# Sparse attention and two gated layers on one core: the planned order of the layers planned anew

## The chip, the cores and the metric

The kernel runs on one core of a Trainium2 chip. The metric is the device time of one execution in microseconds (us); of several executions the median is given. The profile comes from one further execution, and its times are that execution's own.

## The reference

Attention keeps, in each row, the scores within `tau` of the row's maximum, and its output goes through two gated layers, all in float32:

```python
scores = scale * np.matmul(q, k.transpose(0, 1, 3, 2))       # 4 x 8 heads, 576 x 576, head size 64
thresh = np.max(scores, axis=-1, keepdims=True) - tau
scores = np.where(scores >= thresh, scores, -1000000000.0)
...
x = np.ascontiguousarray(attn_out.transpose(0, 2, 1, 3)).reshape(B * S, H * D)    # 2304 x 512
h = x @ w_in                                                 # 512 x 2048
g = h * np.tanh(log1p(exp(h)))
x = g @ w_out
g = x @ w_gate                                               # 512 x 1536
x = (g * sigmoid(g) * (x @ w_val)) @ w_out2
```

## The kernel before

**Two parts.** `attention` works on 16 pairs of heads, about 16.4 us each. `moes` then computes the two feed-forward layers in 30 blocks: layer 1 has 4 groups of hidden columns, layer 2 has 6, and each group meets three row chunks r = 0, 1, 2 of 768 tokens. So blocks 0 to 11 are layer 1 and blocks 12 to 29 layer 2, and a new group of weights is needed at blocks 0, 3, 6, ... 27. All matmuls are in a float32 that is split into a high and a low part (L515 and L519 for weights, L609 and L610 for inputs, L815 and L818 for hidden values g), three products for one.

**The first product of a block** (L783, into PSUM `ha` and `hb`) is done with seven products in place of eight, by sums of quarters of the weights and of the input. The inputs' seven pieces are `B11`, `T1` and so on. They are made once for each layer and chunk (a subtraction at L604, the split at L609 and L610, in tile `xp`), stored to DRAM (L613) and, for later groups, fetched again (L748). ACT copies results out of PSUM (L794: `s` and `u`), DVE adds them (L804 and others: `c`), ACT applies the nonlinearity (L827), and the split gives `g`. **The second product** (L907 in layer 1, L909 in layer 2, into PSUM `y`) is added into `acc` in SBUF, by ACT as a copy in a layer's first group (L923) and by DVE after that (L925).

**A weight's way** (`Weights.convert`). Weights lie in DRAM as 64-bit words of float64 bits. A block of 128 x 512 is loaded into `raw` (two slots, DMA on SP's queue, L480). ACT reads each word's two halves (`cu` L484, `cl` L488), DVE takes the sign (L492) and puts sign and body together (L495, `cn`), and GpSimd adds the rest (L498). Two such blocks, a pair, are then combined on DVE (L546, `sb`) into the sums that the seven products need and split into `wa`, `wb` and `wc` (three slots each); a block of the second product's weights becomes `wo` (six slots). The weights of the first two pairs are made during attention.

**What sets the order.** No engine's order is written by hand. `Plan` gets every operation with an engine, a cost, what it comes after, which slots it takes and frees, and a rank. `Plan.order` runs a list scheduler: at each step the engine that can start earliest takes, among the operations ready within `wait` (`MWAIT` in `moes`) of that time, the one of lowest rank. Operations are then issued in order of planned start. Engines and SP's DMA queue execute in that order, so an operation whose input comes later than planned holds up all behind it. In attention the ranks are numbers in `RANK` and the order is strict (an engine takes them by rank alone). In `moes` a matmul of block b has as its rank its place in time `R` (blocks laid end to end by the matmuls' lengths); evacuations have `R - 40`, piece preparations `R - LEAD`, fetches `R - FETCH` (60). Conversions are ranked by `prepare(bn)`, spread from the start of block bn - 3 to that of block bn:

```python
def rank(s, at=at):
    return T0 + PREP[0] + (T1 - T0 + PREP[1]) * at / n + PRANK.get(s, 0)
```

Here `at` counts the blocks of weights of the group, 0 to n - 1, and `s` is the step (`l` load, `h` high part, `o` low part, `s` sums). In the plan a load costs 1.6 us and its data is there 1.9 us after that; a conversion's add on GpSimd costs 1.1 us.

**The last v.** In attention each pair's v is loaded (L79) into the tile `vn`, of which there is one: the load waits until the product with the pair before's v (`av`, L177) is done.

Of the kernel before, what the change touches and what calls it, by code (L numbers as in the profile page):

```python
# [8 lines left out]
F32 = mybir.dt.float32  # L9
# [7 lines left out]
P = 128  # L17
# [26 lines left out]
def attention(tc, cst, q, k, v, x, beside, S=576):  # L44
# [9 lines left out]
    NP = q.shape[0]  # L54
# [8 lines left out]
    pw = ctx.enter_context(tc.tile_pool(name="a_w", bufs=2, reuse_waits="tile"))  # L63
# [6 lines left out]
    def mine(nm, h):  # L70
        return slice(64, 640) if nm == "k" and h == 0 else slice(0, 576)

    def load(p, nm):
        src = dict(q=q, k=k, v=v)[nm][p]
        if nm == "v":
            t = pw.tile([P, 10, 64], F32, tag="vn", name=f"vn{p}", bufs=SLOTS["vn"])
        else:
            t = pn.tile([P, KW], F32, tag="n", name=f"{nm}n{p}", bufs=SLOTS["n"])[:, 0:src.shape[1]]
        nc.sync.dma_start(out=t, in_=src)  # L79
        st[p][nm + "n"] = t  # L80
# [185 lines left out]
    turns = []  # L266
# [5 lines left out]
    plan = Plan(SLOTS, WAIT)  # L272
    for p in range(NP):
# [17 lines left out]
            op("ACT", .573 + .053 * (nm == "k"), inputs, nm, "hi", key=(nm, "hi"), after=[("q", "scale") if nm == "q" else ("k", "load")], take=[nm])  # L291
            op(*(("Pool", 1.4 + .15 * (nm == "k"), inputs, nm, "lo", nc.gpsimd) if p else ("DVE", .75, inputs, nm, "lo", nc.vector)), key=(nm, "lo"), after=[(nm, "hi")], free=["n"])
        op("Pool", .8, tails, key=("t",), after=[("q", "stack", 1) if p else ("q", "lo", 1)], take=["qt"], free=["q"] * (p > 0))
        op("DMA", 1.3, load, "v", key=("v", "load"), take=["vn"])
        for nm, cost in (("q", 1.3), ("k", 2.6)) * (p > 0):
            for h in range(2):
                op("DMA", cost, stack, nm, h, key=(nm, "stack", h), after=[(nm, "lo"), ("q", "stack", 0)][:2 if (nm, h) != ("q", 0) else 1], take=["stk"] * ((nm, h) == ("q", 0)))
        for i in range(9):
            c, h = divmod(i, 2)
            made = [(y, "stack", z) for y in "qk" for z in ([h] if i < 8 else [0, 1])] if p else [("q", "lo", h if i < 8 else 1), ("k", "lo")]  # L300
            op("PE", .53 if p and i < 8 else .81, scores, i, key=("S", i), after=made + [("t",)] * (i == 8), take=["s"], free=["k", "qt", "stk"] if i == 8 else [])
            op("DVE", .68, rowmax, i, key=("R", i), after=[("S", i)] + [("R", 0)] * (i > 0), take=["sm"] * (i == 0))
            op("Pool", .26, thresh, i, key=("H", i), after=[("R", i)])
            op("ACT", .7, expo, i, key=("E", i), after=[("R", i)], take=["e"])
            op("DVE", .8, mask, i, key=("M", i), after=[("E", i), ("H", i)] + [("M", i - 1)] * h, take=["pp"] if h == 0 else [], free=["s", "e"])
            for m0, n in (((0, 3),), ((3, 3), (6, 3)))[h] if i < 8 else ((0, 4), (4, 2)):
                g = turns[p, "T", next(small)]
                op("PE", .11 * n, trans, c, m0, n, key=("T", c, m0), after=[("M", i)], take=[g] + ["pt"] * (m0 == 0 and c in (0, 2)), free=["pp"] * (m0 == (6 if c < 4 else 4)))
                op("ACT", .365 if c < 4 else .54 if m0 == 0 else .21, evac, c, m0, n, key=("V", c, m0), after=[("T", c, m0)], free=[g])
            if i in (3, 8):  # L310
                u = int(i == 8)
                op("Pool", .26, added, u, key=("P", u), after=[("M", 3)] if u == 0 else [("M", 7), ("M", 8)])
                op("DVE", .2, recip, u, key=("Q", u), after=[("P", u)])
                op("Pool", .38 + .2 * u, rwide, u, key=("rw", u), after=[("Q", u)], take=["rw"], free=["sm"] * u)
                g = turns[p, "T", next(small)]
                op("PE", .22 + .22 * u, rbc, u, key=("B", u), after=[("rw", u)], take=[g], free=["rw"])
                op("ACT", .31, rcopy, u, key=("C", u), after=[("B", u)], take=["rs"], free=[g])
                ready = [("V", y, z) for y in ((0, 1), (2, 3))[u] for z in (0, 3, 6)] + [("V", 4, 0), ("V", 4, 4)] * u + [("v", "load")]
                for n, (j0, j1) in enumerate(PARTS):
                    end = j1 == 5  # L320
                    op("PE", (.432, .538)[u] * (j1 - j0), av, u, j0, j1, key=("A", u, n), after=ready, take=[] if n else [turns[p, "A", u]], free=(["pt"] + ["vn"] * u) * end)
                    ready = [("A", u, n)]
                op("DVE", .335 + .067 * u, xout, u, key=("x", u), after=[("C", u)] + ready, free=[turns[p, "A", u], "rs"])

# [7 lines left out]
class Plan:  # L332
# [37 lines left out]
    def order(self, ops, strict):  # L370
        made = {o["key"]: o for o in ops}
        took = {x: o for o in ops for x in o["take"]}
        gave = {x: o for o in ops for x in o["free"]}
        for o in ops:
            o["t"], o["then"] = 0.0 if strict or o["eng"] != "DMA" else AHEAD, []
        for o in ops:
            before = [(made[x], True) for x in o["after"] if x not in self.given]
            for x, k in o["take"]:
                if (x, k - 1) in took:
                    before.append((took[x, k - 1], False))  # L380
                if k >= self.slots[x]:
                    before.append((gave[x, k - self.slots[x]], True))
            o["left"] = len(before)
            for y, late in before:
                y["then"].append((o, late))
# [7 lines left out]
        while True:  # L393
# [20 lines left out]
                ready[e].remove(o)  # L414
            n += 1
            o["t"], o["at"] = t, n
            clock[e] = t + o["cost"]
            if e == "PE":
                clock[e] += TURN * (turn != (o["key"][1] == "A"))
                turn = o["key"][1] == "A"  # L420
            for y, whole in o["then"]:
                if whole:
                    y["t"] = max(y["t"], clock[e] + self.LAT[e][y["eng"]])
                else:
                    y["t"] = max(y["t"], t)
                y["left"] -= 1
                if not y["left"] and not tight(y):
                    ready[y["eng"]].append(y)
# [16 lines left out]
AHEAD = -20.0  # L445
# [3 lines left out]
AFTER = 10, 20  # L449
TURN = 0.16  # L450
KW = 640
SLOTS = dict(raw=2, wcu=1, wcl=2, wcn=3, sb=1, wa=2, wb=2, wc=2, xo=1, sm=4, s=3, g=2, e=4, pp=3, pt=2, rw=4, rs=3, q=2, k=2, qt=2, vn=1, stk=2, n=2)

PERIOD = 16.3760

# [4 lines left out]
class Weights:  # L460
# [9 lines left out]
            had = self.fixed.setdefault(nm, [])  # L470
            had.append(pool.tile([P, *shape], F32R, name=f"{nm}{len(had)}"))

    def convert(self, plan, pool, src, key, rank, cost=1.0, wait=(), into=None):
        nc, V = self.nc, self.nc.vector
        m, j, rows = src
        raw, up, low, n = plan.new("raw"), plan.new("wcu"), plan.new("wcl"), plan.new("wcn")
# [24 lines left out]
        for s, (eng, t, fn, deps, take, free) in dict(  # L501
            l=("DMA", 1.6 * cost, load, "", [raw], []),
            a=("ACT", .52 * cost, rebias, "l", [up], []),
            b=("ACT", .52 * cost, rest, "l", [low], []),
            c=("DVE", .335 * cost, sign, "l", [n], []),
            d=("DVE", .602 * cost, body, "abc", [], [raw, up]),
            x=("Pool", 1.1 * cost, whole, "bd", [], [low]),
        ).items():
            plan.op(eng, t, fn, K(s), [K(y) for y in deps] + list(wait) * (s == "l"), take, free, rank(s))
        return n  # L510

    def split(self, plan, key, tile, src, dst, n, low, rank, after, take=(), free=()):
# [107 lines left out]
def moes(tc, cp, acc, W, early, where, w_in, w_out, w_gate, w_val, w_out2, out):  # L620
# [36 lines left out]
    def prepare(bn):  # L657
# [15 lines left out]
        n = sum(2 if x[0] == "pair" else 1 for x in order)  # L673
        at = 0
        for what, q, x in order:
            def rank(s, at=at):
                return T0 + PREP[0] + (T1 - T0 + PREP[1]) * at / n + PRANK.get(s, 0)
            if what == "pair":
                ns = [W.convert(plan, pm, src, key, rank, into=pr) for src, key in x]
                weights["u", L, q] = W.combine(plan, pm, ("u", L, q), [key for _, key in x], ns, SENG, WLOW, rank)  # L680
                at += 2
            else:
                src, key = x
                nn = W.convert(plan, pm, src, key, rank if bn or at > 1 else lambda s: FIRST if s == "l" else rank(s), into=pr)
                weights[key] = W.out(plan, pm, key, nn, WLOW, rank)
                at += 1

    n1 = [("E", 1, 3, 2, q, i) for q in layers[1][-1] for i in range(4)]
    for bn, b in enumerate(blocks):
# [38 lines left out]
        for i, (k, q) in enumerate(seq):  # L728
# [3 lines left out]
            if q == g[0]:  # L732
# [8 lines left out]
                if new:  # L741
                    new.turn(plan, piece, PENG, ready, R - LEAD)
                    new.split(plan, piece, room, PLOW, ready, R - LEAD, 1, [xp])
                    new.store(plan, piece, room, R)
                    got = ("x", L, r, piece, "")
                else:
                    def fetch(room=room, piece=piece, L=L, r=r):
# [51 lines left out]
            def summed(nm, src, held, key, deps, free, q=q, tiles=tiles):  # L799
# [5 lines left out]

                S[nm, q] = t
                plan.op("DVE", dS(C), go, key, deps, [t], [S[held, q], *free], R)

            def split(nm, j, s, after, q=q, tiles=tiles):
                g_ = plan.new("g")  # L810
# [44 lines left out]
            elif k == 4:  # L855
# [4 lines left out]
                else:  # L860
                    def times(q=q, tiles=tiles):
                        V.tensor_tensor(out=tiles["c11", q], in0=tiles["A", q], in1=tiles["c11", q], op=ALU.mult)

                    plan.op("DVE", dS(C), times, ("V", *B, q, 0), [(*e, 3), K(4, q)], [], [ha[q]], R)
                    split("c11", q, 0, [("V", *B, q, 0)])
            elif k == 2:
                summed("c11", "B", "s1", ("c11", *B, q), [K(2, q), ("s1", *B, q)], [hb[q]])
# [10 lines left out]
        for s in (1, 0):  # L878
            ys = {}
            for jj, d, c0, c1 in [(jj, d, c0, c1) for jj, d in loop for c0, c1 in (((0, 256), (256, 512)) if ending and s == 0 and d == 2 else ((0, 512),))]:  # L880
# [51 lines left out]
                else:  # L932
                    after.append(("S", L, gi - 1, r, s, d))
                plan.op("ACT" if b["first"] else "DVE", aS(n_) if b["first"] else dS(n_), total_, key, after, [], [ys[d]] * (c1 == 512), R - 40)
                if b["last"] and L == 2:
                    def store(d=d, s=s, r=r, c0=c0, c1=c1):
                        t0 = 2 * C * r + C * s + P * d
# [8 lines left out]
FETCH = 60  # L946
FIRST = -1000
STAGED = (2, 0),
SLATE = 0
LEAD = 15  # L950
MWAIT = 0.06
MSLOTS = dict(ha=2, hb=2, y=4, xp=6, wa=3, wb=3, wc=3, wo=6, raw=2, wcu=2, wcl=2, wcn=3, sb=1, s1=2, u2=2, s5=2, c=4, g=9)
LAG = {1: .85, 2: .9}
PREP = (-5.0, -10.0)
PRANK = dict(l=-6, h=0, o=0)
PIECE = dict()
GLOW = {1: "DVE", 2: "DVE"}
SENG, WLOW, PENG, PLOW = "DVE", "DVE", "DVE", "DVE"
# [118 lines left out]
```

## Time and profile before

| | us |
|---|---|
| median of 3 runs | 1090.65 |
| lowest and highest | 1089.6, 1091.18 |
| the profiled execution's own time | 1085.61 |
| its span, first to last instruction | 1083.7 |
| busy: TensorE, DVE, ACT, GpSimd | 1059.2, 765.5, 651.2, 278.4 |
| granted TensorE clock | 1.000 of 2.4 GHz throughout |

PE is TensorE (PEld its weight loads), POOL is GpSimd, SP the queue that issues the DMAs. The first 281 us of the span are attention, the rest `moes`. Times within the trace count from the span's start. L12 is line 12 of the kernel before; tile names stand as out<-in.

### The profile page before, as it was taken

The page shows a single profiled execution, that of the slowest core. Times are in us where ns is not written, and L with a number is a line of the kernel's source. Part 1 is how long each engine was busy: PE and PEld are TensorE (multiplying, and loading weights), DVE is VectorE, ACT ScalarE, POOL GpSimd, SP SyncE. Part 2 cuts the span into 40 slices and gives each one's busy share as a digit, 9 for nine tenths or more (in the row PEclk, how much of TensorE's full clock was granted, in tenths as well). Part 3 has the DMA queues.
Part 4 walks back from the last instruction along what each step waited for, and adds up shares of the span by engine and source line. Part 5 has one row for each costly group of instructions (what it writes and reads, how often), then busy time and mean ns, then how long its engine had stood idle before and what let it go on. Part 6 is the DMA issues. An engine that isn't in the chain of part 4 may idle for free.

```text
span 1083.7 us, 17927 instructions
## 1 busy us (share of the span) xinstructions
PE 1059.2 (98%) x6358; PEld 970.0 (90%) x6358; DVE 765.5 (71%) x1445; ACT 651.2 (60%) x1313; POOL 278.4 (26%) x467
## 2 busy tenths in 40 slices
PE   6999999999999999999999999999999999999998
PEld 5777777777789999999999999898999999999997
DVE  7888988888686574466377677867487585775645
ACT  6899888887686764355356456656255354453331
POOL 5576877763240110031022002112011020110000
PEclk9999999999999999999999999999999999999999
DMA  5777767763966766576577497789788788887793
GB/s 151 193 189 216 189 166 220 205 200 102 363 242 259 250 239 204 182 273 239 175 246 255 161 337 272 278 291 323 242 292 309 241 316 281 277 293 239 235 304 128
DMA packets 66330, 259.47 MB, mean 239 GB/s; under 512 B 8768, under 2 KB 9024, under 8 KB 66240
## 3 DMA queue, kind: packets, MB, share of 16 engines
q1 hardware_dynamic: 66240, 258.31, 71.9%
q8 instruction: 51, 0.84, 0.3%
q14 instruction: 39, 0.32, 0.1%
HBM read 193.99 MB, written 37.75 MB: 214 GB/s over the span
## 4 chain that ended last, share of the span: by engine, by line
PE 84%; DVE 5%; DMA 3%; ACT 3%; POOL 2%; issue 1%; DVEq 0%; SPq 0%; POOLq 0%; ACTq 0%
PE ha L783 20%; PE y L907 16%; PE hb L783 15%; PE y L909 13%; PE av L177 7%; PE tg L154 6%; PE s L92 5%; DMA raw<-in_dram 2%; PE s L101 2%; DVE sm L109 1%; DVE g L818 1%; PE rg L202 1%; POOL cn L498 1%; DVE c L804 1%; POOL xo L610 1%
## 5 line engine op out<-in xcount | busy, mean ns | idle before, releaser
L498 POOL TENSOR_TENSOR cn<-cn,cl 128x512 int32<-128x512 int32 x68 | 102.5, 1509 | 633.4 <-DVE cn L495 520.6
L907 PE MATMUL y<-g,wo 128*128 128x384 f32 x1152 | 228.5, 334 | 4.1 <-ACT acc L923 3.6
L907 PEld LDWEIGHTS y<-g,wo 128*128 128x128 f32 x1152 | 202.1, 188 | 5.4 <-ACT acc L923 4.6
L909 PE MATMUL y<-wo,g 128*128 128x512 f32 (+1 forms) x654 | 167.4, 392 | 1.5 <-DVE acc L925 0.8
L925 DVE TENSOR_TENSOR acc<-y,acc 128x512 f32<-128x512 f32 (+2 forms) x163 | 100.0, 624 | 92.6 <-PE y L909 59.8
L783 PE MATMUL ha<-xp,wb 128*128 128x384 f32 x720 | 138.9, 335 | 1.1 <-ACT u L794 1.1
L909 PEld LDWEIGHTS y<-wo,g 128*128 128x128 f32 x654 | 120.3, 188 | 21.4 <-ACT xp L609 1.1
L783 PE MATMUL hb<-xp,wb 128*128 128x384 f32 x720 | 138.9, 335 | 0.5 <-ACT s L794 0.5
L783 PEld LDWEIGHTS ha<-xp,wb 128*128 128x128 f32 x720 | 126.5, 188 | 4.9 <-ACT u L794 1.9
L783 PEld LDWEIGHTS hb<-xp,wb 128*128 128x128 f32 x720 | 126.1, 188 | 2.9 <-ACT s L794 1.4
L818 DVE TENSOR_TENSOR g<-c,g 128x384 fp32r<-128x384 f32 x168 | 102.0, 610 | 30.5 <-ACT g L815 30.5
L127 DVE SCALAR_TENSOR_TENSOR pp<-s,sm,e 128x576 f32<-128x576 f32 x144 | 115.1, 813 | 10.9 <-ACT e L119 6.1
L815 ACT CAST g<-c 128x384 fp32r<-128x384 f32 x168 | 85.9, 512 | 53.2 <-DVE c L851 28.3
L109 DVE TENSOR_REDUCE sm<-s 128x1 f32<-128x576 f32 x144 | 106.6, 751 | 15.0 <-PE s L92 12.0
L827 ACT ACTIVATE c<-c 128x384 f32<-128x384 f32 x144 | 75.6, 525 | 60.9 <-DVE c L804 60.5
L119 ACT ACTIVATE e<-s,sm 128x576 f32<-128x576 f32 x144 | 105.7, 754 | 5.3 <-DVE sm L109 4.4
L154 PE MATMUL tg<-idf,pp 128*128 128x128 f32 x656 | 102.3, 280 | 2.8 <-DVE pp L127 1.7
L160 ACT COPY pt<-tg 128x384 f32<-128x384 f32 x192 | 87.3, 489 | 27.7 <-PE tg L154 26.6
L92 PE MATMUL s<-stk 128*128 128x320 f32 x480 | 93.0, 316 | 0.7 <-issue 0.5
L794 ACT COPY u<-ha 128x384 f32<-128x384 f32 x60 | 28.8, 480 | 103.2 <-PE ha L783 103.2
L154 PEld LDWEIGHTS tg<-idf,pp 128*128 128x128 f32 x656 | 73.1, 141 | 18.6 <-ACT e L119 5.8
L177 PE MATMUL av<-pt,vn 128*64 128x256 f32 (+1 forms) x640 | 84.7, 411 | 0.0
(95 smaller groups left out, 1555.0 us busy)
## 6 DMA issues: line engine op xcount, KB each, us to landing
raw<-in_dram SPq DMA_DIRECT2D x68, 512.0 KB, 5.5
xp<-x20T SPq DMA_DIRECT2D x24, 768.0 KB, 5.7
xp<-x21T SPq DMA_DIRECT2D x20, 768.0 KB, 5.5
xp<-x22T SPq DMA_DIRECT2D x20, 768.0 KB, 5.9
xp<-x20B SPq DMA_DIRECT2D x18, 768.0 KB, 5.8
xp<-x10T SPq DMA_DIRECT2D x16, 768.0 KB, 5.2
xp<-x21B SPq DMA_DIRECT2D x15, 768.0 KB, 5.8
xp<-x22B SPq DMA_DIRECT2D x15, 768.0 KB, 5.9
```

Source lines behind the costliest of these rows:

```text
L92: nc.tensor.matmul(out=s[:, c0:c0 + n], lhsT=d["stk"][:, 0, q0:q0 + P], rhs=d["stk"][:, w, k0:k0 + n], start=w == 1, stop=w == 2)
L109: nc.vector.tensor_reduce(out=d["nm"][:, i:i + 1], in_=d["s", i], op=ALU.max, axis=AX.X, negate=True)
L119: nc.scalar.activation(out=e, in_=d["s", i], func=AF.Exp, bias=d["nm"][:, i:i + 1])
L127: nc.vector.scalar_tensor_tensor(out=d["pp", c][:, 576 * h:576 * h + 576], in0=d["s", i], scalar=d["th"][:, i:i + 1], in1=d["e", i], op0=A ...
L154: nc.tensor.transpose(g[:, 128 * m:128 * m + 128], d["pp", c][:, o:o + 128], idf)
L177: nc.tensor.matmul(out=d["av", u][64 * h:64 * h + 64, 0:n], lhsT=d["vn"][:, 5 * h + j], rhs=d["pt", u][:, 5 * h + j if j < 4 else 4, 0:n], ...
L498: nc.gpsimd.tensor_tensor(out=self.n[key], in0=self.n[key], in1=self.l[key], op=ALU.add)
L783: nc.tensor.matmul(out=tiles[bank, q], lhsT=w[:, a, w0 + P * d:w0 + P * d + P], rhs=x[:, z, d], start=k in (1, 5, 2) and d == 0 and y == 0 ...
L818: (V if GLOW[L] == "DVE" else nc.gpsimd).tensor_tensor(out=tiles["g", j, s][:, 1], in0=tiles[nm, q], in1=f(tiles["g", j, s][:, 0]), op=ALU ...
L907: nc.tensor.matmul(out=y[:, 0:C], lhsT=w[:, a, P * d:P * d + P], rhs=h[:, x], **m)
L909: nc.tensor.matmul(out=y[:, c0:c1], lhsT=h[:, x, P * d:P * d + P], rhs=w[:, a, c0:c1], **m)
L925: V.tensor_tensor(out=a, in0=y, in1=a, op=ALU.add)
```

## The change

The two-layer part has the same operations as before; what differs is how they are ranked and what the planner assumes.

- `LATE`, `PREP` and `PRANK`: the conversions of blocks 3, 6, 9, 12 and 15 begin to rank 40, 20, 60, 30 and -10 us later, within the same end; start and end shift from (-5, -10) to (0, -4), the loads' own lead of 6 goes, and high and low parts and sums get later ranks.
- `HOLD`: a load may be held until its rank less `HOLD`; with the number given, it never is.
- `SLACK`: outside attention, whatever follows a weight's load is planned 5 us later.
- `PORT`: outside attention, an operation on DVE that does not read PSUM is planned longer by 1.5 times its overlap with GpSimd's current operation, one on GpSimd by 0.3 times its overlap with DVE's.
- A slot counts as free when all operations that free it are done (before: the last one listed), and the store of a piece is now one of them. Stores rank `SOON` = 13 us earlier, pieces `LEAD` = 13 in place of 15, those staged for layer 2 8 us later (`SLATE`).
- `MWAIT` is 0.2 in place of 0.06, `LAG[1]` (where in a block the second product's ranks begin) 0.87 in place of 0.85.
- Attention: pair 15's v has a tile of its own, `vz`.

```diff
+    def vslot(p):
+        return "vz" if p == NP - 1 else "vn"
...
-            t = pw.tile([P, 10, 64], F32, tag="vn", name=f"vn{p}", bufs=SLOTS["vn"])
+            t = pw.tile([P, 10, 64], F32, tag=vslot(p), name=f"vn{p}", bufs=SLOTS["vn"])
...
-        gave = {x: o for o in ops for x in o["free"]}
+        gave = {}
         for o in ops:
-            o["t"], o["then"] = 0.0 if strict or o["eng"] != "DMA" else AHEAD, []
+            for x in o["free"]:
+                gave.setdefault(x, []).append(o)
+        for o in ops:
+            o["t"], o["then"] = max(0.0 if strict or o["eng"] != "DMA" else AHEAD, o.get("hold", -1e9)), []
...
-                    before.append((gave[x, k - self.slots[x]], True))
+                    before += [(y, True) for y in gave[x, k - self.slots[x]]]
...
-            clock[e] = t + o["cost"]
+            cost = o["cost"]
+            if not strict and e in ("DVE", "Pool"):
+                if e == "DVE" and not o.get("psum"):
+                    cost += PORT[0] * min(cost, max(0.0, clock["Pool"] - t))
+                elif e == "Pool":
+                    cost += PORT[1] * min(cost, max(0.0, clock["DVE"] - t))
+            clock[e] = t + cost
...
-                    y["t"] = max(y["t"], clock[e] + self.LAT[e][y["eng"]])
+                    y["t"] = max(y["t"], clock[e] + self.LAT[e][y["eng"]] + (SLACK if e == "DMA" and o["key"][0] == "w" and not strict else 0.0))
...
+            late = LATE.get(bn, 0.0)
+
             def rank(s, at=at):
-                return T0 + PREP[0] + (T1 - T0 + PREP[1]) * at / n + PRANK.get(s, 0)
+                return T0 + late + PREP[0] + (T1 - T0 - late + PREP[1]) * at / n + PRANK.get(s, 0)
+
+            hold = rank("l") - HOLD if bn else None
...
-                    new.store(plan, piece, room, R)
+                    new.store(plan, piece, room, R - SOON, [xp])
...
-SLATE = 0
-LEAD = 15
-MWAIT = 0.06
+HOLD = 1000000000.0
+LATE = {3: 40, 6: 20, 9: 60, 12: 30, 15: -10}
+PORT = 1.5, 0.3
+SLATE = 8
+SOON = 13
+SLACK = 5.0
+LEAD = 13
+MWAIT = 0.2
...
-LAG = {1: .85, 2: .9}
-PREP = (-5.0, -10.0)
-PRANK = dict(l=-6, h=0, o=0)
+LAG = {1: 0.87, 2: 0.9}
+PREP = 0.0, -4.0
+PRANK = {'l': 0, 'h': 0, 'o': 6, 's': 9}
```

## Rows read from the trace of the kernel before

**Rows 1.** The page's first part: busy time, share of the span, instructions.
```profile
PE 1059.2 (98%) x6358; PEld 970.0 (90%) x6358; DVE 765.5 (71%) x1445; ACT 651.2 (60%) x1313; POOL 278.4 (26%) x467
```
**Rows 2.** TensorE by stretch: from:to, length, busy (matmuls started), clock, DMA share, GB/s.
```profile
281.20:336.10 54.90, 48.75 (x271) 1.00 0.73 278
340.00:640.00 300.00, 300.00 (x1732) 1.00 0.68 233
660.00:680.00 20.00, 19.15 (x111) 1.00 0.71 273
740.00:760.00 20.00, 19.38 (x100) 1.00 0.91 331
```
**Rows 3.** Stretches of all engines: length, busy of PE, PEld, DVE, ACT, POOL (instructions).
```profile
281.20:312.60 31.40, 28.87 (x161) 27.43 (x160) 26.69 (x40) 25.61 (x50) 11.62 (x6) 1.00 0.74 283
312.60:336.10 23.50, 19.88 (x112) 18.92 (x111) 21.84 (x37) 18.89 (x38) 5.80 (x4) 1.00 0.71 271
375.00:469.00 94.00, 94.00 (x543) 93.78 (x542) 50.57 (x91) 49.04 (x99) 12.73 (x8) 1.00 0.65 217
```
**Rows 4.** Timeline near 318 us: start, length, instruction, [idle before <- what ended it].
```profile
317.05 1.04 ACT L515 CAST wb<-sb 128x1024 fp32r<-128x1024 f32 x1 [2.07 <-DVE sb L546]
...
318.83 1.32 PE L907 MATMUL y<-g,wo 128*128 128x384 f32 x6 [1.85 <-ACT acc L923]
```
**Rows 5.** Chain that ended last, in order of time: start, us, a load's landing.
```profile
283.99 7.64 DMA raw<-in_dram
```
**Rows 6.** Timeline near 292 us, ACT and TensorE.
```profile
291.71 0.67 ACT L484 ACTIVATE cu<-raw 128x512 f32<-128x512 f32 x1 [1.41 <-DMA raw<-in_dram]
...
292.81 1.31 PE L783 MATMUL ha<-xp,wb 128*128 128x384 f32 x6 [1.14 <-ACT u L794]
```
**Rows 7.** Timeline near 295 and 301 us: GpSimd's add and DVE's subtraction.
```profile
295.22 1.29 POOL L498 TENSOR_TENSOR cn<-cn,cl 128x512 int32<-128x512 int32 x1 [6.69 <-ACT cl L488]
...
295.58 1.35 DVE L818 TENSOR_TENSOR g<-c,g 128x384 fp32r<-128x384 f32 x1 [1.17 <-ACT g L815]
...
301.19 0.55 DVE L818 TENSOR_TENSOR g<-c,g 128x384 fp32r<-128x384 f32 x1
```
**Rows 8.** GpSimd's groups from 281 to 337 us: busy, mean ns, idle before.
```profile
L498 POOL TENSOR_TENSOR cn<-cn,cl 128x512 int32<-128x512 int32 x9 | 17.4, 1940 | 33.7 <-DVE cn L495 18.9 <-ACT s L794 7.4 <-ACT cl L488 6.7
```
**Rows 9.** Stretches of DVE's L495 (first), then L546 and L519, with POOL's column.
```profile
305.00:331.20 26.20, 3.40 (x5) 1.00 0.71 263
...
312.60:331.20 18.60, 3.98 (x8) 0.00 (x0) 1.00 0.66 245
...
312.60:331.20 18.60, 2.91 (x4) 0.00 (x0) 1.00 0.66 245
```
**Rows 10.** DVE's groups from 281 to 337 us: busy, mean ns, idle before.
```profile
L492 DVE TENSOR_SCALAR cn<-raw 128x512 int32<-128x512 int32 x9 | 4.6, 526 | 0.3 <-DMA raw<-in_dram 0.3
```
**Rows 11.** Timeline from 253 to 279 us, around the last v.
```profile
253.43 16.06 SPq L79 DMA_DIRECT2D vn<-in_dram  x2
...
272.95 2.38 PE L177 MATMUL av<-pt,vn 128*64 128x256 f32 x20
...
278.43 0.43 ACT L210 COPY rs<-rg 128x320 f32<-128x320 f32 x1 [0.40 <-PE rg L204]
```
**Rows 12.** SP's waits over the span: us in total, times, longest.
```profile
SPq L748 <- PE ha L783: 292.8, 93, 8.4
...
SPq L613 <- DVE xp L610: 77.1, 32, 8.0
```
**Rows 13.** Timeline near 744 us, and a weight's way from 726 to 739 us.
```profile
743.99 0.70 ACT L484 ACTIVATE cu<-raw 128x512 f32<-128x512 f32 x1 [1.54 <-DMA raw<-in_dram]
...
746.35 1.65 DVE L851 TENSOR_TENSOR c<-c 128x384 f32<-128x384 f32 x1
...
726.25 2.25 SPq L480 DMA_DIRECT2D raw<-in_dram  x2
...
738.83 0.69 DVE L519 TENSOR_TENSOR wa<-cn,wa 128x512 fp32r<-128x512 f32 x1 [0.32 <-ACT wa L515]
```

More of the change, by code (lines that the diff above doesn't have):

```diff
@@ L293, in attention @@
         op("Pool", .8, tails, key=("t",), after=[("q", "stack", 1) if p else ("q", "lo", 1)], take=["qt"], free=["q"] * (p > 0))
-        op("DMA", 1.3, load, "v", key=("v", "load"), take=["vn"])
+        op("DMA", 1.3, load, "v", key=("v", "load"), take=[vslot(p)])
         for nm, cost in (("q", 1.3), ("k", 2.6)) * (p > 0):
@@ L320, in attention @@
                     end = j1 == 5
-                    op("PE", (.432, .538)[u] * (j1 - j0), av, u, j0, j1, key=("A", u, n), after=ready, take=[] if n else [turns[p, "A", u]], free=(["pt"] + ["vn"] * u) * end)
+                    op("PE", (.432, .538)[u] * (j1 - j0), av, u, j0, j1, key=("A", u, n), after=ready, take=[] if n else [turns[p, "A", u]], free=(["pt"] + [vslot(p)] * u) * end)
                     ready = [("A", u, n)]
@@ L451 @@
 KW = 640
-SLOTS = dict(raw=2, wcu=1, wcl=2, wcn=3, sb=1, wa=2, wb=2, wc=2, xo=1, sm=4, s=3, g=2, e=4, pp=3, pt=2, rw=4, rs=3, q=2, k=2, qt=2, vn=1, stk=2, n=2)
+SLOTS = dict(raw=2, wcu=1, wcl=2, wcn=3, sb=1, wa=2, wb=2, wc=2, xo=1, sm=4, s=3, g=2, e=4, pp=3, pt=2, rw=4, rs=3, q=2, k=2, qt=2, vn=1, vz=1, stk=2, n=2)
 PERIOD = 16.3760
@@ L471, in add, with convert @@
             had.append(pool.tile([P, *shape], F32R, name=f"{nm}{len(had)}"))
-    def convert(self, plan, pool, src, key, rank, cost=1.0, wait=(), into=None):
+    def convert(self, plan, pool, src, key, rank, cost=1.0, wait=(), into=None, hold=None):
         nc, V = self.nc, self.nc.vector
@@ L509, in convert @@
             plan.op(eng, t, fn, K(s), [K(y) for y in deps] + list(wait) * (s == "l"), take, free, rank(s))
+            if s == "l" and hold is not None:
+                plan.ops[-1]["hold"] = hold
         return n
@@ L675, in prepare @@
         for what, q, x in order:
+            late = LATE.get(bn, 0.0)
             def rank(s, at=at):
-                return T0 + PREP[0] + (T1 - T0 + PREP[1]) * at / n + PRANK.get(s, 0)
+                return T0 + late + PREP[0] + (T1 - T0 - late + PREP[1]) * at / n + PRANK.get(s, 0)
+            hold = rank("l") - HOLD if bn else None
             if what == "pair":
-                ns = [W.convert(plan, pm, src, key, rank, into=pr) for src, key in x]
+                ns = [W.convert(plan, pm, src, key, rank, into=pr, hold=hold) for src, key in x]
                 weights["u", L, q] = W.combine(plan, pm, ("u", L, q), [key for _, key in x], ns, SENG, WLOW, rank)
@@ L683, in prepare @@
                 src, key = x
-                nn = W.convert(plan, pm, src, key, rank if bn or at > 1 else lambda s: FIRST if s == "l" else rank(s), into=pr)
+                nn = W.convert(plan, pm, src, key, rank if bn or at > 1 else lambda s: FIRST if s == "l" else rank(s), into=pr, hold=hold)
                 weights[key] = W.out(plan, pm, key, nn, WLOW, rank)
@@ L807, in summed @@
                 plan.op("DVE", dS(C), go, key, deps, [t], [S[held, q], *free], R)
+                plan.ops[-1]["psum"] = True
             def split(nm, j, s, after, q=q, tiles=tiles):
@@ L864, in moes @@
                     plan.op("DVE", dS(C), times, ("V", *B, q, 0), [(*e, 3), K(4, q)], [], [ha[q]], R)
+                    plan.ops[-1]["psum"] = True
                     split("c11", q, 0, [("V", *B, q, 0)])
@@ L934, in moes @@
                 plan.op("ACT" if b["first"] else "DVE", aS(n_) if b["first"] else dS(n_), total_, key, after, [], [ys[d]] * (c1 == 512), R - 40)
+                plan.ops[-1]["psum"] = True
                 if b["last"] and L == 2:
```

## Prediction

> **What bounds the kernel now.** First the page's busy row: TensorE is busy 98% of the span [rows 1], so a new order can only give back the time in which TensorE waits. Then TensorE by stretch. In the even middle (340 to 640 us) it is busy all of 300 us and starts 1732 matmuls, 0.1732 us each [rows 2]. From 281.2 to 336.1 us, where the two-layer part begins, it starts 271 in 54.9 us. 271 x 0.1732 = 46.9, so about 8.0 us are lost there, though the busy column shows only 54.9 - 48.75 = 6.2 idle (a matmul's modelled end covers part of each gap). Its two largest gaps later are 0.85 us idle at 660 to 680 and 0.62 at 740 to 760 [rows 2]. So some 8.0 + 1.5 = 9.5 us, 0.9%, can be won in the part whose order changes. I take the first 281 us as unchanged: attention's operations are ordered strictly by their ranks, which stay, and the port's price is left out of strict planning.
>
> **Why TensorE waits.** In the window table of all engines DVE is busy 21.84 of 23.5 us in the second half of that stretch, but 50.57 of 94 later [rows 3]: the work is bunched. The timeline gives three causes.
> - ACT, in order, stands behind a weight conversion. The cast of wb waits 2.07 us for DVE's sb, the evacuation of y stands behind it, and TensorE waits 1.85 us for that [rows 4].
> - A weight load lands late: 7.64 us from its issue [rows 5]. ACT waits 1.41 us with it at the head of its queue, the copy of u stands behind, TensorE idles 1.14 [rows 6].
> - GpSimd holds up DVE. The subtraction that makes g's low part takes 0.55 us alone and 1.35 beside the conversion's add on GpSimd [rows 7], and a matmul that reads it stands behind.
>
> **The change, part by part.** No operation is added or taken away in the two-layer part, so engine time stays; the order moves.
>
> *Conversions later (LATE, PREP, PRANK).* Nine conversions run on GpSimd in the stretch [rows 8]. Four are the w_out blocks of block 0, needed at once; five belong to block 3. A block of this layer is 180 matmuls, 180 x 0.1732 = 31.2 us, so block 3 starts 93.6 us after block 0. Before, its conversions' ranks are -5 + 83.6 x at/8, with `at` 0 and 2 for its two pairs: -5 and 15.9, ahead of the piece preparations of block 1 (31.2 - 15 = 16.2 and up). After, they are 40 + 49.6 x at/8: 40 and 52.4, behind nearly all of those (31.2 - 13 = 18.2 to 45) and behind block 1's own evacuations (31.2 - 40 = -9 to 20). Each engine takes the ready operation of lowest rank, so the five conversions fall back into block 2, where there is room. HOLD is 1e9, so nothing is really held back; ranks only decide between ready operations.
> What leaves the stretch on DVE, for those five: bodies 3.40 (x5), sb 3.98 (x8), low parts 2.91 (x4) [rows 9], and signs 5 x 0.526 = 2.6 [rows 10], together 12.9 us. Some 11 of them lie in the second half (23.5 us: all of sb and of the low parts, three bodies and signs), where DVE would fall from 93% to about 46%, and ACT is freed of their two copies and a cast each. The loss there is 23.5 - 112 x 0.1732 = 4.1 us [rows 3] (two matmuls on a boundary count in both halves). Its cause goes; some piece preparations still land late. I take 3.3 back (bounds 0 and 4.1: nearer the second, since the even middle, with DVE at 54%, loses nothing [rows 2, 3]).
>
> *Loads planned 5 us later (SLACK).* The plan had a load usable 1.6 + 1.9 = 3.5 us after its issue and now 8.5. The late one took 7.64 [rows 5], so the operations behind it would no longer stand behind an unfinished load. I take 1.2 us (0 to 1.4).
>
> *GpSimd overlap counted (PORT).* A DVE operation is planned longer by 1.5 times what it overlaps. For 0.55 us that is 0.83, where the trace shows 0.80 [rows 7]. This removes no collision; it lets other work be put ahead. The other losses of the first half (31.4 - 161 x 0.1732 = 3.5 us, less the 1.2) are 2.3; I take 0.8 back (0 to 2.3), as the four conversions of block 0 stay there.
> The Trainium skill, "SBUF — State Buffer", section "Who interferes with whom", says that the pair of ports is an exclusive lock, held for a whole instruction, so that the second to issue fully blocks. By that rule the stretched 1.35 us is a wait for the add's end, as the trace shows (295.22 + 1.29 = 296.51, and the subtraction ends at 296.93 [rows 7]), and it does not grow with the waiting operation's length.
>
> *Own buffer for the last v (vz).* The load of the last v waits at the head of SP's queue, whose two issues of v take from 253.43 to 269.49 us, and the first weight loads stand behind it. But TensorE's product with that v starts at 272.95 without a wait for it, and ACT can take up a weight only behind attention's last copy, at 278.43 [rows 11]. I cost it at nothing. If that cover were gone, an earlier weight could save at most ACT's gap of 0.40 before that copy. Bounds: 0 and 0.4 gained.
>
> *Stores earlier (SOON), pieces later (LEAD 13, SLATE 8), LAG, MWAIT, slots freed by both readers.* SP runs in order: a store planned 13 us earlier may stand there waiting for DVE's low part (8.0 us at the longest so far), with weight loads and fetches behind it; fetches already wait 292.8 us in 93 waits for a slot [rows 12] while TensorE is full. I cost this at nothing, covered by fetches that rank 60 us ahead of their use; without that cover one such wait costs up to 8.0. SLATE touches the 0.85 us at 679, which I take as the bound either way. MWAIT lets the plan leave an engine idle up to 0.2 us for a preferred operation instead of 0.06. I put that and new collisions at 0.5 us lost: between 0, since the even middle idles 0.00 in 300 us [rows 2], the nearest row, and 3, if one in forty of TensorE's 912 groups of matmuls (12 x 46 + 18 x 20) waits 0.14 us longer.
>
> *The two later stalls.* At 744 us a late load keeps ACT waiting 1.54, then an add on GpSimd stretches a DVE product to 1.65 [rows 13], and TensorE idles 0.62 [rows 2]. SLACK reaches this: 0.6 back (0 to 0.6). The one at 679 us I leave.
>
> **Sum:** 3.3 + 1.2 + 0.8 + 0.6 - 0.5 = 5.4 us, 0.5%. The profiled execution took 1085.61 us, with 1083.7 of span and 1.9 around it; it is 5.0 below the median of the runs, 1090.65. I carry the difference over unscaled: profiled 1080.2, median about 1085.2, and round to 1085.0.
>
> **Rivals.**
> 1. *Nearly all comes back.* If the filler work fits wherever TensorE leaves room, 9.5 us go: 1081.2. For it: DVE at 54% later [rows 3]. Against it: block 0 keeps its four conversions and ACT its 25.61 us of work in 31.4 [rows 3].
> 2. *The lock is undercharged.* A short DVE operation that comes right after GpSimd's start waits the whole 1.29 us, where the plan adds 0.83 to one of 0.55: 0.46 short each time. Over the four conversions that stay in the first stretch that is 1.8 us not recovered: 5.4 - 1.8 = 3.6, so 1087.0. That is what the skill's lock rule (same page and section) would make of it; the trace agrees so far as [rows 7] go.
> 3. *The bound is the amount of work.* In block 0 ACT and DVE are at 82% and 85% [rows 3]. If pieces and evacuations merely take the conversions' place as what is late, the stalls move by a block and stay, and only the late load's 1.2 us are saved: 1089.5, within 0.2%.
> 4. *Slower: weights late at a group's start.* Conversions that yield to everything may be done only when block 3, 6, 9, 12 or 15 needs them. From a load's issue at 726.25 to wa's low part, done at 739.52, are 13.3 us [rows 13]. A third of that bare at three of the five starts costs 13.3 us: 1085.2 + 13.3 = 1098.5. It decides when the low part of a group's first wa ends after the block's first matmul could start. Against it: before, all of block 3's conversions that are moved lie before 336 us [rows 8], some 40 us ahead of the block at 281.2 + 93.6 = 375, and conversions start whenever raw and a target slot are free.
> That the change does nothing is out, since the ranks that it changes order most of the work.
>
> **Chances.** Forecast (4 to 7 us won) 0.40, rival 1 0.20, rival 2 0.13, rival 3 0.13, rival 4 0.14. A measurement of this kernel can tell about 0.2%, 2.2 us, from no change. Faster by more: 0.40 + 0.20 + 0.13 = 0.73; within it 0.13; slower 0.14. The range of 1080.5 to 1091.5 takes in the first four cases with their bounds and leaves out rival 4 and a thin end of rival 1, near 0.2. The forecast's own range is 1083.5 to 1086.7.
>
> **What would show it.** In the changed profile: the adds on GpSimd between 281 and 336 us fall from nine to four or five; DVE in the second half falls from 21.84 us to 12 to 17; TensorE starts 295 to 305 matmuls in those 54.9 us instead of 271; ACT no longer waits over 1 us for a raw load ahead of a copy that TensorE needs; the even middle keeps 300.00 busy. I am wrong if TensorE idles behind wa or wo at a group's start, if the middle shows gaps, or if the first stretch loses as much with fewer conversions in it.

## The result, and the profile after

The changed kernel takes 1077.55 us (median of 4 runs, 1076.44 to 1078.89) against 1090.5 (median of 4): a ratio of 0.9882, interval 0.9865 to 0.9899. Measured again with the experiments, beside 11 new runs of before (1083.73 to 1090.43), it is 1077.31 us and 0.991 (0.9891 to 0.9928). The forecast was 1085.0, a gain of about 5.5 us: right in its sign and too small in its size. The measured 1077.55 us lie below the range that was given (1080.5 to 1091.5).

First the length of the two-layer part. A timeline row shows its first matmul in the changed kernel; the line above it is the head of the view, with the span:

```profile
core 0 of [0], span 1076.1 us
...
283.22 2.35 PE L801 MATMUL ha<-xp,wa 128*128 128x384 f32 x12
```

From that matmul to the end are 1076.1 - 283.22 = 792.9 us. In the profile of before they were 1083.7 - 281.17 = 802.5. This length is the measure in all that follows: it leaves out attention, whose end lies anywhere from 281.1 to 284.3 us in the profiles, whichever kernel it is (last section). So the prediction's "first 281 us as unchanged" holds for the order of the work, not for its time in a single execution. TensorE by stretch, the columns as in [rows 2]:

```profile
283.22:338.10 54.88, 53.76 (x308) 1.00 0.69 255
340.00:640.00 300.00, 300.00 (x1733) 1.00 0.69 242
660.00:680.00 20.00, 20.00 (x113) 1.00 0.50 170
740.00:760.00 20.00, 20.00 (x107) 1.00 0.87 301
```

In the first stretch 308 matmuls start where 271 did, so 54.88 - 308 x 0.1732 = 1.5 us are lost instead of 8.0. Both later gaps are closed, and the middle is as full as before. All engines in the two halves of that stretch and later, the columns as in [rows 3]:

```profile
283.22:314.60 31.38, 30.25 (x172) 29.45 (x171) 26.74 (x39) 25.09 (x48) 7.00 (x5) 1.00 0.69 264
314.60:338.10 23.50, 23.50 (x138) 23.50 (x137) 21.54 (x33) 19.23 (x38) 4.97 (x4) 1.00 0.69 244
377.00:471.00 94.00, 94.00 (x545) 94.00 (x544) 53.66 (x96) 49.99 (x98) 10.96 (x9) 1.00 0.65 221
```

The second line is the surprise. DVE is about as full as it was (21.54 us of 23.5, before 21.84), and yet TensorE doesn't wait at all. GpSimd's group in the stretch, to be set against [rows 8], shows that eight of the nine conversions are still there:

```profile
L510 POOL TENSOR_TENSOR cn<-cn,cl 128x512 int32<-128x512 int32 x8 | 12.0, 1496 | 47.2 <-DVE cn L507 37.9 <-ACT s L812 8.6 <-ACT wo L529 0.7
```

What did move is a part of the work that combines a pair (`sb`). Its operations on DVE, then ACT and GpSimd, in the second half of the stretch, in before and then in the changed kernel:

```profile
312.57:336.07 23.50, 5.19 (x9) 1.04 (x1) 0.00 (x0) 1.00 0.71 270
```

```profile
314.62:338.12 23.50, 2.81 (x5) 1.05 (x1) 0.00 (x0) 1.00 0.69 244
```

Other work took its place, so DVE stayed full. The crowding that the prediction read as the main cause did not go away, and did not have to.

### The profile page after: what moved, and what is told of

Same layout as the page of the kernel before. It is cut to its first block, busy times and chain, and to the rows that moved or that the text cites. A ratio compares the mean times of both kernels' runs of the same rounds, so it can differ in the third digit from the quotient of the medians.

```text
span 1076.1 us, 17949 instructions
## 1 busy us (share of the span) xinstructions
PE 1057.3 (98%) x6358; PEld 972.2 (90%) x6358; DVE 775.1 (72%) x1445; ACT 655.5 (61%) x1313; POOL 269.3 (25%) x467
## 4 chain that ended last, share of the span: by engine, by line
PE 89%; POOL 3%; ACT 2%; DVE 2%; DMA 2%; issue 2%; SPq 1%; DVEq 0%; POOLq 0%; ACTq 0%
PE ha L801 22%; PE y L927 18%; PE hb L801 17%; PE y L929 14%; PE av L180 6%; PE tg L157 5%; PE s L95 5%; PE s L104 1%; DVE sm L112 1%; DMA stk<-qh 1%; DVE pp L130 1%; PE rg L205 1%; DMA x10T<-xo 0%; POOL xo L624 0%; SPq L240 0%
## 5 line engine op out<-in xcount | busy, mean ns | idle before, releaser
L510 POOL TENSOR_TENSOR cn<-cn,cl 128x512 int32<-128x512 int32 x68 | 94.3, 1387 | 632.7 <-DVE cn L507 443.4
L837 DVE TENSOR_TENSOR g<-c,g 128x384 fp32r<-128x384 f32 x168 | 104.6, 623 | 34.7 <-ACT g L834 34.0
```

Of the source, the lines that this page charges most:

```text
L510: nc.gpsimd.tensor_tensor(out=self.n[key], in0=self.n[key], in1=self.l[key], op=ALU.add)
L837: (V if GLOW[L] == "DVE" else nc.gpsimd).tensor_tensor(out=tiles["g", j, s][:, 1], in0=tiles[nm, q], in1=f(tiles["g", j, s][:, 0]), op=ALU ...
```

## The experiments

Each takes one part of the change alone, leaves one out, or goes after one suspected cost. "Two-layer part" is the span less the start of its first matmul.

| run | what it is | ratio to before (95%) | span, first ha | two-layer part |
|---|---|---|---|---|
| b_again | before | 1.0003 (0.999 to 1.0016) | 1085.7, 283.65 | 802.0 |
| b_slack | before + SLACK | 0.9956 (0.994 to 0.9972) | 1081.8, 283.61 | 798.2 |
| b_port | before + PORT | 0.9961 (0.9949 to 0.9973) | 1079.9, 281.24 | 798.7 |
| b_late | before + LATE, PREP, PRANK | 1.0001 (0.9986 to 1.0016) | 1084.0, 282.31 | 801.7 |
| a_again | after | 0.991 (0.9891 to 0.9928) | 1075.4, 282.55 | 792.9 |
| a_noslack | after without SLACK | 0.9936 (0.9918 to 0.9954) | 1077.4, 281.22 | 796.2 |
| a_noport | after without PORT | 0.9932 (0.9914 to 0.9951) | 1078.1, 282.67 | 795.4 |
| a_nolate | after without LATE, PREP, PRANK | 0.9918 (0.9901 to 0.9935) | 1075.5, 281.69 | 793.8 |
| b_slack_port | before + SLACK + PORT | 0.9921 (0.9909 to 0.9933) | 1076.5, 281.60 | 794.9 |
| a_norest | after without the small edits | 0.9916 (0.9901 to 0.9932) | 1075.6, 281.56 | 794.0 |
| b_noadd | before, GpSimd's add left out | 0.9949 (0.9933 to 0.9965) | 1079.1, 281.12 | 798.0 |
| a_lock | after, whole lock priced | 0.9908 (0.9893 to 0.9923) | 1077.3, 284.31 | 793.0 |
| b_slack2 | before + SLACK of 2 | 0.9964 (0.9952 to 0.9976) | 1083.3, 283.43 | 799.9 |
| b_slack10 | before + SLACK of 10 | 0.9939 (0.9925 to 0.9953) | 1078.7, 281.33 | 797.4 |

The two-layer part repeats well: 802.5 and 802.0 for before, 792.9 twice for after. It moves with the order and hardly with the execution, with one exception: in the profiles of b_slack and b_late a stretch at TensorE's lower clock adds some 1.2 and 1.4 us (last section).

### Before again, and one part at a time

> The kernel before, unchanged. The profiled execution of before took 1085.61 us against timed runs of 1089.6 to 1091.2, so about 5 us of the 13 gained are not in the two profiles. Theory A (the old order is fragile: loads that land later in other executions stop ACT and DVE): this profile comes out near 1090 and the 4 to 5 us more lie in the two-layer part, behind raw loads. Theory B (the start differs from execution to execution, attention included): the two-layer part is again near 802 us and the difference lies before 285 us. Time against itself: 1.000.

Theory B holds. The two-layer part is the same, and so are its main stalls. TensorE's three largest waits in it are these, the first being the 3.6 us that ACT's evacuations cost; in before the same three are 3.6, 0.8 and 1.1 us.

```profile
PE y L907 <- ACT acc L923: 3.6, 3, 1.8
PE y L909 <- DVE acc L925: 0.9, 1, 0.9
PE ha L783 <- ACT u L794: 0.8, 1, 0.8
```

In both profiles the stalls therefore belong to the planned order and the usual durations, not to a chance delay.

```diff
+SLACK = 5.0
-                    y["t"] = max(y["t"], clock[e] + self.LAT[e][y["eng"]])
+                    y["t"] = max(y["t"], clock[e] + self.LAT[e][y["eng"]] + (SLACK if e == "DMA" and o["key"][0] == "w" and not strict else 0.0))
```

> Before, with SLACK alone (loads of weights planned 5 us later). Theory A: most of the gain, 6 to 9 us faster (1082 to 1085), TensorE's stalls behind ACT cu gone. Theory C (the bunching of block 3's conversions is the cause): 1 to 2 us faster, the stalls from 312 to 336 us stay. Theory D (collisions of DVE and GpSimd): within 1 us.

4.1 us come from this line alone (802.3 - 798.2, 802.3 being the mean of the two profiles of before): less than theory A's 6 to 9, more than C's 1 to 2. One stall of 1.86 us is left, and the lower clock behind it costs this profile another 1.2, so the order alone may be worth some 5. Waits for raw loads over the span, in before, then in b_slack, where ACT has none left to list:

```profile
ACT cu L484 <- DMA raw<-in_dram: 30.8, 28, 4.5
DVE cn L492 <- DMA raw<-in_dram: 12.0, 13, 2.9
```

```profile
DVE cn L492 <- DMA raw<-in_dram: 1.6, 2, 0.9
```

```diff
+PORT = 1.5, 0.3
-            clock[e] = t + o["cost"]
+            cost = o["cost"]
...
+            clock[e] = t + cost
```

(the lines between are those of the change, and operations on DVE that read PSUM are marked as there)

> Before, with PORT alone (overlap of DVE and GpSimd counted in the plan). Theory D: most of the gain, 6 to 9 us faster, with the first stretch's loss of 8 us down to 3. Theory C or A: 0 to 2 us faster. The prediction's term was 0.8.

3.6 us, between the two expectations: a cause of about the size of the late loads, but not the only one. It lies in the first stretch, where 294 matmuls start in 54.9 us (before 271), a loss of 4.0 us instead of 8.0.

```diff
+LATE = {3: 40, 6: 20, 9: 60, 12: 30, 15: -10}
-PREP = (-5.0, -10.0)
-PRANK = dict(l=-6, h=0, o=0)
+PREP = 0.0, -4.0
+PRANK = {'l': 0, 'h': 0, 'o': 6, 's': 9}
```

> Before, with LATE, PREP and PRANK alone (conversions ranked later). Theory C: the second half of the first stretch loses under 1 us instead of 4, 3 to 5 us faster, DVE there falls to 12 to 17 us of 23.5. Theory A: under 2 us, because the late loads still stop ACT. Theory D: under 2 us.

Theory C, the prediction's largest term, falls: a ratio of 1.0001. Leaving out the lower clock, the order is worth 2.0 us at most (0.6 + 1.4). The conversions did not leave: eight of the nine adds on GpSimd are still in the stretch. The adds, then the half in which DVE should have become free, all engines, and the longest wait that remained (L909 of this run is L907 of before):

```profile
L498 POOL TENSOR_TENSOR cn<-cn,cl 128x512 int32<-128x512 int32 x8 | 15.6, 1956 | 35.9 <-ACT cl L488 15.4 <-ACT s L796 7.4 <-ACT c L829 6.3
```

```profile
313.71:337.20 23.49, 20.96 (x114) 20.64 (x113) 23.16 (x37) 17.50 (x35) 6.87 (x4) 0.93 0.83 295
```

```profile
PE y L909 <- ACT acc L925: 2.5, 1, 2.5
```

DVE is at 23.16 us of 23.49. The scheduler gives a likely reason: a rank orders operations that are ready at the same moment, and a conversion's step whose raw slot is free may be the only one ready and is then taken whatever its rank. How often that is so, no run shows.

### One part less

> The changed kernel as it is, on the chip of the runs below and beside new runs of before. From its first ha matmul to the end it took 792.9 us where before took 802.6 and 802.0. If the two-layer part is all that differs, the ratio is 1 - 9.5/1087.6 = 0.9913; if the first measurement (0.9882) holds, 3 us more come from somewhere the profiles don't show.

The first case: the 9.4 us of the two-layer part (802.3 - 792.9) explain 0.991.

> The changed kernel with SLACK = 0. Sum theory (each part takes away its own stalls, SLACK alone gave 4 us of the two-layer part): two-layer part 796 to 797.5 us. Interplay theory (with the other parts in, the loads are no longer what is late): under 795.

3.3 us are lost again (796.2) and the waits for raw loads come back, larger than in before: the sum theory's lower end.

```profile
ACT cu L496 <- DMA raw<-in_dram: 48.7, 33, 3.4
DVE cn L504 <- DMA raw<-in_dram: 16.2, 12, 2.4
```

> The changed kernel with PORT = 0, 0. Sum theory (PORT alone gave 3.6 us): two-layer part 796 to 797. Interplay theory: either under 795 (SLACK's room hides the collisions) or over 798 (late conversions collide more).

2.5 us lost, between the sum theory and the interplay theory; TensorE waits 1.2 us for the low part of wo and 1.0 at the change of layers.

> The changed kernel with LATE empty and PREP and PRANK as before. Sum theory (LATE alone gave 0.5 us): two-layer part 793 to 794. Theory that later conversions pay only in a plan that has loads and collisions right: 795.5 to 798, with new stalls from 312 to 336 us.

0.9 us lost, the sum theory's case. Its ratio and that of a_again overlap, so the timing alone can't tell the two apart.

### Two parts together, and what is left

> Before, with SLACK and PORT and nothing else. From its first ha matmul to the end before takes 802.3 us, SLACK alone 798.2, PORT alone 798.7, the whole change 792.9. If the two remove different stalls they add up: 794 to 795.5. If they remove the same ones: 797 to 798.5. If it is below 793.5, the other edits (LATE and the small ones) bring nothing.

They add up: 802.3 - 794.9 = 7.4 us, against 4.1 + 3.6 = 7.7. By the ratios it is 0.79% against 0.44% and 0.39%. Counted without the lower clock in b_slack's profile, the two single gains overlap by some 1.5 us. Two assumptions of the plan, in some ten lines, carry four fifths of the 9.4 us.

```diff
-LEAD = 13
-MWAIT = 0.2
+LEAD = 15
+MWAIT = 0.06
...
-                    new.store(plan, piece, room, R - SOON, [xp])
+                    new.store(plan, piece, room, R)
```

(a_norest; LAG, SLATE and the rule on freeing as before, too)

> The changed kernel with SLATE, LEAD, MWAIT, LAG, SOON and the rule for freeing slots as before; SLACK, PORT, LATE and vz stay. Additive theory: the single removals gave back 3.3 (SLACK), 2.6 (PORT) and 1.0 (LATE) of 9.4 us, so 2.5 are left for these edits: 795 to 795.8. Interplay theory (no part is needed twice): under 794.

1.1 us lost, neither 2.5 nor nothing. Nearly all of it is one stall, at the change from layer 1 to layer 2, which the changed kernel doesn't have:

```profile
PE y L926 <- ACT s L809: 1.0, 1, 1.0
```

Which of the small edits closes it was not tried. Here too the ratios overlap, and the medians are the same (1077.28 and 1077.31 us), so the 1.1 us rest on the profiles alone.

### The collisions themselves

```diff
         def whole():
-            nc.gpsimd.tensor_tensor(out=self.n[key], in0=self.n[key], in1=self.l[key], op=ALU.add)
+            pass
```

> Before, in its own order, with the GpSimd add of each conversion left out (so the weights lack their lowest bits and the kernel leaves that part of the computation out); the plan still counts it. Theory that collisions of DVE and GpSimd are worth what PORT brought: two-layer part 797.5 to 799.5, the subtraction for g stays at 0.55 us, the waits for raw loads stay near 30 us. Theory that PORT only reshuffles: 800.5 to 802.

798.0: with the order unchanged, the adds on GpSimd cost 4.3 us of TensorE's time, about what PORT wins (the conversion's chain also becomes shorter by the add, and this run can't separate the two; the waits for raw loads even rose, ACT's to 40.7 us and DVE's to 27.0). The subtraction for g, all 168 of the two-layer part, in b_noadd, b_again, b_port and after:

```profile
L818 DVE TENSOR_TENSOR g<-c,g 128x384 fp32r<-128x384 f32 x168 | 92.2, 552 | 32.2 <-ACT g L815 32.0
```

```profile
L818 DVE TENSOR_TENSOR g<-c,g 128x384 fp32r<-128x384 f32 x168 | 100.7, 602 | 32.0 <-ACT g L815 31.9
```

```profile
L825 DVE TENSOR_TENSOR g<-c,g 128x384 fp32r<-128x384 f32 x168 | 101.3, 608 | 33.0 <-ACT g L822 32.9
```

```profile
L837 DVE TENSOR_TENSOR g<-c,g 128x384 fp32r<-128x384 f32 x168 | 104.6, 623 | 34.7 <-ACT g L834 34.0
```

The mean is 552 ns without the add, 602 with it (610 in the first profile of before), 608 with PORT alone and 623 in the changed kernel. So PORT does not make these collisions fewer. That they now fall where the plan has left room for them would fit, but no row shows it one by one.

```diff
-                    cost += PORT[0] * min(cost, max(0.0, clock["Pool"] - t))
+                    cost += max(0.0, clock["Pool"] - t)
...
-                    cost += PORT[1] * min(cost, max(0.0, clock["DVE"] - t))
+                    cost += max(0.0, clock["DVE"] - t)
...
-            x=("Pool", 1.1 * cost, whole, "bd", [], [low]),
+            x=("Pool", 1.29 * cost, whole, "bd", [], [low]),
```

> The changed kernel with the plan's price of an overlap set to the whole rest of the other engine's operation (an exclusive lock), and the add on GpSimd planned at 1.29 us in place of 1.1. Rival 2 of the prediction (the lock is undercharged): the 1.7 us that the two-layer part still loses fall to under 1, 791 to 792. If the share of 1.5 is close enough: 792.5 to 794.5, no difference that can be measured.

793.0, no difference that can be measured: rival 2 falls as a reason for time lost. For PORT, unlike for SLACK below, no series of sizes was run. That its gain comes from the priced collisions rests on b_noadd, on b_port and on a_noport.

### Is it the late landing, or any other order?

> Before, with SLACK = 2 alone: a load is planned as usable 5.5 us after its issue, the median landing of raw in the profile. Theory that SLACK works because loads land late: the waits of ACT and DVE for raw loads, 43 us in total before and none of note with 5, are between, 5 to 25 us, and the two-layer part between 798.2 and 802.3. Theory that SLACK only makes another order, good by chance: the waits stay over 30 us, or the two-layer part is off that line.

> Before, with SLACK = 10 alone: usable 13.5 us after issue, later than any landing seen (7.6). Theory of late loads: nothing more to win over SLACK = 5, two-layer part 797.5 to 800, no waits for raw loads; a loss only where the two raw slots now turn over too slowly in the plan. Theory of another order: anywhere from 795 to 804.

With a slack of 0, 2, 5 and 10 us, the two-layer part is 802.3, 799.9, 798.2 and 797.4 us, and the waits for raw loads of ACT and DVE together 42.8, 7.3, 1.6 and none. At 2 us they are:

```profile
DVE cn L492 <- DMA raw<-in_dram: 4.0, 3, 2.2
ACT cu L484 <- DMA raw<-in_dram: 3.3, 4, 1.4
```

Both go the same way, and little is left after 5, as the theory of late loads has it (the 0.8 us from 5 to 10 are less than the lower clock costs b_slack). They are not proportional. The sum of such waits is no price by itself either: with PORT alone it is 60.9 us and in a_noslack 64.9, and both are faster than before. What counts is whether a chain that TensorE needs stands behind the wait. Also, single stalls come and go with each order (b_slack10 has a wait near 700 us, PE ha <- DVE c, 0.4 us, that b_slack has not), so single edits are read to about 1 us.

## Why the prediction was wrong

- **"Conversions later ... I take 3.3 back"** is the step that failed. Alone it brought 0.6 us of the two-layer part and a ratio of 1.0001; left out of the change it cost 0.9. The prediction said itself that ranks only decide between ready operations, and then let the conversions "fall back into block 2" all the same. And it took a full engine for the reason of the wait. Its 4.1 us of the second half were real, but the other two parts win them. All engines in that half, in b_slack, b_port, b_slack_port and a_nolate, the first three with all ranks as before:

```profile
315.01:338.51 23.50, 23.32 (x125) 23.32 (x126) 21.47 (x35) 18.25 (x38) 4.79 (x4) 0.93 0.79 284
```

```profile
312.64:336.14 23.50, 22.29 (x128) 21.69 (x127) 22.80 (x39) 21.03 (x43) 4.43 (x3) 1.00 0.56 204
```

```profile
313.00:336.50 23.50, 23.44 (x135) 23.12 (x134) 22.22 (x37) 20.15 (x41) 6.07 (x4) 1.00 0.65 254
```

```profile
313.09:336.59 23.50, 23.50 (x137) 23.36 (x136) 21.12 (x37) 19.43 (x37) 6.27 (x4) 1.00 0.64 218
```

Matmuls go from 112 (and 114 with LATE alone) to 125, 128, 135 and 137, while DVE stays between 21.1 and 22.8 us. With SLACK and PORT together 23.50 - 135 x 0.1732 = 0.1 us of the 4.1 is left.
- **"I take 1.2 us (0 to 1.4)" and 0.6 for SLACK** were too small: 4.1 alone, 3.3 in the change. The term counted the two stalls that have a raw load right ahead of them. But ACT and DVE wait 42.8 us for raw loads over the span, and SLACK also ends stalls that carry another name: "ACT acc" is TensorE's largest wait in before, and between 325 and 340 us it costs b_again 1.8 us in two waits and b_slack nothing. That late loads had displaced the work in front of these is the likely link; it was not followed wait by wait.
- **"I take 0.8 back (0 to 2.3)" for PORT** was too small: 3.6 alone, 2.5 in the change. Its mechanism held as far as the means tell (collisions are not removed). The bound was wrong, since it looked at the first half alone: there PORT brings 168 matmuls where before has 161, some 1.2 us and within the bounds, but in the second half 128 where before has 112, some 2.8 us, and that half had been given to later conversions.
- **"0.5 us lost" to MWAIT and new collisions** did not come, and the small edits, costed at nothing, won 1.1 by the profiles.
- **The ceiling of 9.5 us** was too low: 9.4 were won and 1.5 are still lost. The later gaps were taken from idle time, 0.85 and 0.62. From 740 to 760 us 107 matmuls start now where 100 did, and 7 x 20 / 107 = 1.3 us. The prediction had seen in the first stretch that idle time hides part of a gap and did not carry it over.
- **"I carry the difference over unscaled"** failed too. The profiled execution of before is 5.0 us below the median of its runs (1085.61 against 1090.65), and the prediction kept that distance. In the changed kernel the two are 1077.86 and 1077.55. So of the 7.5 us between the forecast median and the measured one some 5.3 are this step; for the profiled execution the forecast of 1080.2 was 2.3 us too high, a distance that would be larger if attention had not ended 2.05 us later.
- **vz at nothing** held as far as the trace tells: the first weight loads start 10.84 us ahead of the part's first matmul (272.38 in after) where they did 10.85 ahead (270.32 in before), though v itself no longer waits.
- **Rival 1** (nearly all comes back) is what happened in the two-layer part, though by another way than room on DVE. **Rival 4** (weights late) did not: TensorE's only waits from 283 us on are these, the first in block 0 at 306 us; none is at the start of block 3 or later:

```profile
PE y L927 <- DVE wo L533: 0.7, 1, 0.7
PE hb L801 <- ACT s L812: 0.4, 1, 0.4
```

- Of the 13 us between the first medians, 9.4 are the two-layer part. The other 3.5 did not come back in the second measurement (1086.79 against 1077.31). Before's four runs of the first measurement lie at 1089.6 to 1091.2. Of its 76 later executions (those timed with the experiments), from 1083.6 to 1091.3, only six took 1089.6 or more, so four out of four is hardly chance. What was different then, no run shows.

## What to carry to other kernels

Where a list scheduler writes the order, look first for what it believes and the trace denies: compare its landing time of a load and its durations beside other engines with the rows, and correct these before touching priorities. A full engine next to a waiting one is no cause until the wait is followed to its first late input. And measure lost matmul time by matmuls started in a stretch, for every gap, not by idle time.

## What was not expected of the hardware

**TensorE's start.** The matmuls run at half pace until some time between 11 and 20 us, and when that ends differs between executions of the same order. Two matmuls of 320 columns take 0.54 us at 8.81 in before and 0.30 at 14.38; in b_again they still take 0.53 at 15.79. From 12 to 16 us, in before and then in b_again, TensorE starts 23 and 10 matmuls:

```profile
12.00:16.00 4.00, 2.79 (x23) 1.00 0.17 37
```

```profile
12.00:16.00 4.00, 2.35 (x10) 1.00 0.16 36
```

The clock column says 1.00 in both, so here the pace has to be read from the counts, and the "1.000 of 2.4 GHz throughout" in the table of before doesn't hold for these first microseconds. The two-layer part then began at 281.17 and 283.65 us; over all sixteen profiles, of either order, at 281.1 to 284.3. Of the 2.48 us between the two, 1.71 are there at the first `av` (23.18 and 24.89 us), and the rest grows later in attention. The start alone doesn't decide: a_noport has its first `av` at 23.25 and its two-layer part at 282.67.

**A wait can cost more than its length.** In b_slack, after TensorE had waited 1.86 us, the granted clock fell to its lower level (1.2 GHz) for part of the next 4 us, and 16 matmuls started in which 23 would have:

```profile
314.00:316.50 2.50, 1.31 (x7) 1.00 0.97 318
316.50:320.50 4.00, 4.00 (x16) 0.57 0.97 289
320.50:324.00 3.50, 3.50 (x22) 1.00 1.02 427
```

The same happened in b_late after a wait of 2.53 us (its 0.93 above), where 15 matmuls started in the next 4 us:

```profile
332.66:336.66 4.00, 4.00 (x15) 0.65 0.12 48
```

In before, a wait of 1.85 us [rows 4] had no such sequel. About 7 x 0.173 = 1.2 us were added to a stall of 2 in b_slack, and 8 x 0.173 = 1.4 in b_late.

The same sum shows in runs without a profile. Of the 76 later executions of before, 32 have a mean granted clock of 0.998 or less, as b_slack and b_late have in theirs, and 44 of 0.999 or 1.000. The first took 1088.0 us on average, the others 1086.8. So before pays this price in some executions, though neither of its two profiles caught one. In the nine executions of the changed kernel, whose longest wait in the two-layer part of the profile is 0.7 us, it is never under 0.999.
